# Second mixture layer: three quarters of its tiles in pairs, two raw-weight buffers, one ring of five PSUM banks

## The chip, the cores and the metric

The kernel runs on one core of a Trainium2 chip. The metric is the device time of one execution in microseconds. Before the change three runs gave 902.35, 903.67 and 905.14 us, so the median is 903.67 us.

## The reference, cut to what matters

Three stages follow one another: a gated recurrent attention, a soft mixture of experts, and a second mixture. The change is in the second mixture and in the step that leads into it.

```python
def _moe2_ref(x, w_gate, w1, w2):        # x 3072x320, w1 8x320x1024, w2 8x1024x320
    logits = x @ w_gate
    P = np.exp(logits - logits.max())
    for _ in range(8):                   # Sinkhorn steps over rows and columns
        P /= P.sum(1, keepdims=True) + 1e-09
        P /= P.sum(0, keepdims=True) + 1e-09
        P *= N / E
    for e in range(E):                   # E = 8
        h = np.maximum(x @ w1[e], 0.0)
        out += P[:, e:e + 1] * (h @ w2[e])
```

## The kernel before, in words

x of the second mixture is itself a product of a 3072x32 matrix c with 32 slot rows, so x @ w1[e] is computed as c @ (slots @ w1[e]). The small product slots @ w1[e] is `s1_p` (its matmuls are in `col4`, L1016 and L1022, its PSUM tile is called pu). It is scaled by a power of two and split into float16 parts in the tile sst. The power of two comes from `pow2`, which needs the largest absolute value over all 128 partitions. For that one of two ways is used: an all-reduce on POOL (L1113), or two transfers on SP's queue, the column of 128 maxima to DRAM (col, L1108) and back as a row on all partitions (row, L1109), after which DVE reduces it (`pow2_b`, L1118 to L1126). `pow2_w` does it for the second weights w2, `pow2_s` for s1.

The 3072 rows of x are 24 tiles of 128 rows. For a tile, `z_` (L1508) computes a half of x @ w1[e] into a PSUM bank of the pool psz (3 banks). ACT takes relu of it into float16 (`hi_z`, L1514), DVE the float16 rest (`relu_with`, L1517). The product with w2[e] uses three float16 products: high by high, high by low, low by high.

There are three kinds of units, each a run of slots; a slot is a handful of matmuls of the unit (`consume`), and a `produce` step of a unit that comes later.

- `Old` (4 slots): the last four tiles of expert 0. Expert 0 itself runs in `g1`/`g2` before that, block by block, with the eight Sinkhorn steps beside it on DVE (`sinkhorn`, L1383 to L1398).
- `One` (4 slots): one tile, 24 matmuls of 320 columns (L1540), then one DVE addition into acc (L1560).
- `Two` (7 slots): two tiles i and j at once, by seven products of half size (12 matmuls of 160 columns each, 84 in all, L1635) instead of eight. It needs sums of blocks of h and of w2. Sums of h: ACT casts (`cast`, L1588), DVE sums (L1517 into tmr), one sum on POOL (L1594, from r21 and r22), and five low parts on POOL (`lo_s`, L1520). Sums of w2 per expert: four on POOL (`sum_w`, L1490), then `sum_h` on ACT and `sum_l` on POOL. The result is put together by `keep_m`, `drain_x`, `drain_z` and `drain_y` on DVE and a little ACT.

Per expert 1 to 7 the units are eight times `One, Two`, so 88 slots (PER). `LEAD` says how many slots ahead of its first slot a unit's z halves are produced, 14 for both kinds. In that time the h parts must be ready; opr (two buffers), tmr (one buffer of five parts) and chl (three buffers) hold them. PSUM: psz 3 banks, psy 3 banks (y of One, y of Two), psp 2 banks (x and z of Two, pu).

Beside the units, `plan(c, f)` puts the preparation of the next expert n at slots counted from the expert's first slot. load_w2 brings w2 to the one tile raw at slot 80 of the expert before; `amax` (DVE) at 5 to 9, `pow2_w` at 14 with `pow2_b` 16 slots later, `prep_a` (ACT, high part of w2, at 31 to 34), `prep_s` (ACT scales raw in place, L1712, and POOL takes the low part, L1713), sums of w2 at 54 to 77, s1 at 33 to 54, and `scale_p` (DVE, L1159, the 24 scaled gate weights of an expert) at 78. Expert 1 has no expert before it in this loop, so its preparation is given in `EXTRA`, beside expert 0's blocks, and its sums by `plan_sums(4, 1, ...)` beside the `Old` units. Expert 1's units also multiply acc by the gate weight of expert 0 (`first`, L1555, DVE).

PE, ACT, DVE and POOL run in the order of the program text; SP's queue is ordered by a planner. Each engine takes its instructions strictly in order and waits for data by semaphores.

Of the kernel before, what the change touches and what calls it, by code (L numbers as in the profile page):

```python
# [20 lines left out]
def mlstm_moe_kernel(  # L21
# [984 lines left out]
    psy = ctx.enter_context(tc.tile_pool(name="psy", bufs=3, space=PSUM, reuse_waits="tile"))  # L1006
    psp = ctx.enter_context(tc.tile_pool(name="psp", bufs=2, space=PSUM, reuse_waits="tile"))
# [86 lines left out]

    def pow2(e, a, mx, later=None):
# [4 lines left out]
        iv, sc = (wp.tile([P, 1], F32, tag=f"{n_}{a}", name=f"{n_}{a}", bufs=2) for n_ in ("iv", "sc"))  # L1100
# [13 lines left out]
        pow2_b(e, a, mr, iv, sc)  # L1114
# [99 lines left out]
    def s1_p(e):  # L1214
        tmp["s1"] = psp.tile([P, TB], F32, tag="p", name="pu2")[:, 0:FQ]
# [229 lines left out]
    EXTRA = {2: [(amax, 0)], 3: [(amax, 1)], 4: [(amax, 2)], 5: [(amax, 3)], 7: [(prep_1, 0)], 9: [(prep_1, 1)],  # L1445
             10: [(s1_c, 0), (s1_c, 1)], 12: [(s1_c, 2), (s1_c, 3)], 14: [(prep_1, 2)], 16: [(prep_1, 3)]}
# [129 lines left out]
    class Two(One):  # L1576
        slots, banks = 7, 4
# [36 lines left out]
        def consume(self, k, at):  # L1614
# [18 lines left out]
            for kp in range(KH):  # L1633
                for a, b in ((0, bh), (0, bl), (1, bh)):
# [3 lines left out]
                    )  # L1638
            if k == 2:
# [21 lines left out]
        def drain_y(self):  # L1661
# [15 lines left out]

    units = [Old(tt) for tt in range(TPB)]
    ones_, twos = 0, 0
    for e in range(1, E):  # L1680
        for i in range(0, NT, 3):
            units += [One(e, i, None), Two(e, i + 1, i + 2, twos)]
            units[-2].buf = ones_
            ones_, twos = ones_ + 1, twos + 1
    LEAD = {One: 14, Two: 14}
# [11 lines left out]
    PER = sum(u.slots for u in units[TPB:]) // (E - 1)  # L1697
# [5 lines left out]
    for tt in range(TPB):  # L1703
        st = (NB - 2) * TPB + tt
        plan(4 * tt + 3, sinkhorn, st)
        for op, kk in EXTRA.get(st, ()):
            plan(4 * tt + 3, op, 1, kk)

    def prep_s(e, kk):
        ks = slice(2 * kk, 2 * kk + 2)  # L1710
        t = src2[e][:, ks, :]
        nc.scalar.activation(out=t, in_=t, func=AF.Copy, scale=scw[e][1])  # L1712
        nc.gpsimd.tensor_tensor(out=wl[e][:, ks, :], in0=t, in1=wh[e][:, ks, :], op=ALU.subtract)  # L1713
# [112 lines left out]
```

## Time and profile before

| | us |
|---|---|
| median of three runs | 903.67 |
| the profiled execution, its own time | 898.99 |
| its span | 897.3 |
| PE busy | 862.9 (96%) |
| DVE busy | 716.1 (80%) |
| POOL busy | 588.9 (66%) |
| ACT busy | 558.1 (62%) |

Busy time is a union: where instructions of an engine overlap, it counts once. "Releaser" is what ended an engine's idle time. Expert 0's blocks run from about 207 to 269.5 us, the four `Old` units from 269.5 to 286.9 us, experts 1 to 7 from 286.9 us to the end. The granted TensorE clock is 0.997 of full speed (2.4 GHz) over the span.

### The profile page before, as it was taken

How to read it: one execution, taken by the hardware profiler on the slowest of the kernel's cores; microseconds unless marked ns; L12 is line 12 of the kernel's file. 1: busy time of each engine (PE TensorE's matmuls, PEld its weight loads, DVE VectorE, ACT ScalarE, POOL GpSimd, SP SyncE). 2: the span in 40 equal slices, each digit the busy share in tenths (PEclk: the TensorE clock that was granted, in tenths of full speed). 3: DMA queues.
4: the chain of work that ended last, by engine and by line, in shares of the span. 5: the costliest groups of instructions: out<-in, count | busy, mean ns of one | idle time of the engine just before them, and what ended most of it. 6: DMA issues, size and time to landing. Idle time of an engine off the chain costs nothing.

```text
span 897.3 us, 26669 instructions
## 1 busy us (share of the span) xinstructions
PE 862.9 (96%) x10996; PEld 728.8 (81%) x10996; DVE 716.1 (80%) x1534; ACT 558.1 (62%) x1110; POOL 588.9 (66%) x596
## 2 busy tenths in 40 slices
PE   7999997899998989999999999999999999999997
PEld 5878884356676878888999899989889998988996
DVE  7777875455899989897788788878987897888774
ACT  7656653353245567668766776687577767767662
POOL 5766660000014679967996799689769977997663
PEclk9999999999999999999999999999999999999999
DMA  8999999960100121204110201051100110000111
GB/s 170 173 199 185 191 248 323 326 182 1 55 6 30 31 57 26 60 2 39 45 60 2 66 16 61 5 64 45 31 5 10 40 31 5 19 1 31 46 46 60
DMA packets 136402, 67.11 MB, mean 75 GB/s; under 512 B 105209, under 2 KB 130041, under 8 KB 136281
## 3 DMA queue, kind: packets, MB, share of 16 engines
q1 hardware_dynamic: 136009, 64.92, 30.1%
q8 instruction: 86, 1.41, 0.7%
q14 instruction: 35, 0.29, 0.2%
q10 hardware_dynamic: 224, 0.30, 0.1%
q0 software_dynamic: 48, 0.20, 0.1%
HBM read 60.17 MB, written 5.02 MB: 73 GB/s over the span
## 4 chain that ended last, share of the span: by engine, by line
PE 66%; DVE 10%; DMA 7%; POOL 7%; issue 5%; ACT 3%; SPq 1%; DVEq 0%; POOLq 0%; ACTq 0%
PE y L1540 15%; PE z L1508 6%; POOL op L1520 3%; DMA bigy<-in_moe_w_dram 3%; PE pss L432 2%; DVE tmr L1517 2%; PE ptk L383 2%; PE oa L477 2%; PE y L1312 2%; PE y L1313 2%; PE y L1314 2%; DMA wa<-in_moe_w_dram 1%; POOL raw L1490 1%; PE pe L402 1%; DVE acc L1560 1%
## 5 line engine op out<-in xcount | busy, mean ns | idle before, releaser
L1520 POOL TENSOR_TENSOR op<-tmr,op 128x512 f16<-128x512 f32 x280 | 319.1, 1168 | 22.1 <-ACT op L1588 19.0
L1635 PEld LDWEIGHTS <-op 128*128 128x128 f16 x4704 | 328.3, 98 | 0.6 <-issue 0.5
L1588 ACT CAST op<-tmr 128x512 f16<-128x512 f32 x280 | 170.0, 616 | 108.1 <-DVE tmr L1517 55.7
L1540 PE MATMUL y<-wx,ch 128*128 128x320 f16 x1344 | 219.0, 299 | 0.0
L1517 DVE SCALAR_TENSOR_TENSOR tmr<-z,tmr 128x512 f32<-128x512 f32 x168 | 114.7, 683 | 56.5 <-ACT op L1514 50.0
L1540 PEld LDWEIGHTS <-ch 128*128 128x128 f16 x1344 | 122.7, 98 | 35.0
L1508 PE MATMUL z<-cst,sst 96*128 96x128 f16 x1344 | 131.0, 219 | 11.7 <-DVE tmr L1517 4.9
L1594 POOL TENSOR_TENSOR tmr<-tmr 128x512 f32<-128x512 f32 x56 | 71.2, 1271 | 95.2 <-ACT tmr L1514 95.2
L1508 PEld LDWEIGHTS <-sst 96*128 96x128 f16 x1344 | 100.2, 98 | 33.6 <-issue 11.3
L1514 ACT ACTIVATE tmr<-z 128x512 f32<-128x512 f32 x112 | 64.8, 596 | 63.5 <-PE z L1508 51.7
L1517 DVE SCALAR_TENSOR_TENSOR ch<-z,ch 128x512 f16<-128x512 f32 x112 | 77.0, 688 | 18.1 <-ACT ch L1514 16.6
L1517 DVE SCALAR_TENSOR_TENSOR op<-z,op 128x512 f16<-128x512 f32 x112 | 76.2, 681 | 0.0
L1514 ACT ACTIVATE ch<-z 128x512 f16<-128x512 f32 x112 | 66.1, 591 | 2.8 <-PE my__8101 L1635 1.3
L1514 ACT ACTIVATE op<-z 128x512 f16<-128x512 f32 x112 | 66.6, 595 | 0.1
L1490 POOL TENSOR_TENSOR raw<-raw 128x640 f32<-128x640 f32 x28 | 43.8, 1565 | 8.3 <-DVE acc L1323 7.3
L1314 PE MATMUL y<-wh,hl 128*128 128x320 f16 x160 | 47.8, 299 | 0.3 <-DVE hl L1295 0.3
L1312 PE MATMUL y<-wh,hh 128*128 128x320 f16 x160 | 47.8, 299 | 0.0
L1313 PE MATMUL y<-wl,hh 128*128 128x320 f16 x160 | 47.8, 299 | 0.0
L411 ACT ACTIVATE dd<-pe 128x512 f32<-128x512 f32 x48 | 29.2, 609 | 29.4 <-PE pe L402 28.9
L1294 ACT ACTIVATE hh<-z 128x512 f16<-128x512 f32 x48 | 26.6, 595 | 33.1 <-PE z L1291 32.8
L1713 POOL TENSOR_TENSOR wx<-raw,wx 128x640 f16<-128x640 f32 x24 | 33.6, 1408 | 15.1 <-ACT raw L1712 15.1
L439 DVE TENSOR_TENSOR dd<-pss,dd 128x512 f32<-128x512 f32 x48 | 31.0, 685 | 14.7 <-PE pss L432 11.9
(1078 smaller groups left out, 1653.0 us busy)
## 6 DMA issues: line engine op xcount, KB each, us to landing
wa<-in_moe_w_dram SPq DMA_DIRECT2D x18, 512.0 KB
raw<-in_moe_w_dram SPq DMA_DIRECT2D x28, 320.0 KB
kq<-in_k_dram SPq DMA_DIRECT2D x24, 160.0 KB
kq<-in_q_dram SPq DMA_DIRECT2D x24, 160.0 KB
vz<-in_v_dram SPq DMA_DIRECT2D x24, 160.0 KB
xr<-in_o_gate_dram SPq DMA_DIRECT2D x24, 160.0 KB
wb<-in_moe_w_dram SPq DMA_DIRECT2D x6, 640.0 KB
out_dram<-acc SPq DMA_DIRECT2D x24, 160.0 KB
```

What stands on the lines that cost most here:

```text
L1312: nc.tensor.matmul(y, hh[:, kc, ts], wh[e][:, kc, :], start=(kc == 0), stop=False)
L1313: nc.tensor.matmul(y, hh[:, kc, ts], wl[e][:, kc, :], start=False, stop=False)
L1314: nc.tensor.matmul(y, hl[:, kc, ts], wh[e][:, kc, :], start=False, stop=(kc == KF - 1))
L1490: nc.gpsimd.tensor_tensor(out=quarter(*o), in0=quarter(*a), in1=quarter(*b), op=op)
L1508: nc.tensor.matmul(z[:, k, :], Sst[e][:, kc * P:(kc + 1) * P], cst[:, i * P:(i + 1) * P], start=True, stop=True,)
L1514: nc.scalar.activation(out=o, in_=z, func=AF.Relu)
L1517: nc.vector.scalar_tensor_tensor(out=o, in0=z, scalar=0.0, in1=x, op0=ALU.max, op1=op)
L1520: nc.gpsimd.tensor_tensor(out=o, in0=x, in1=h, op=ALU.subtract)
L1540: nc.tensor.matmul(self.y, self.at(a, kc), b[self.e][:, kc, :], start=(kc == a == 0 and b is wh), stop=(kc == KF - 1 and a == 1),)
L1588: cast = lambda m, x: nc.scalar.copy(out=hi(m), in_=x)
L1594: at(0, lambda: nc.gpsimd.tensor_tensor(out=s1_, in0=r21, in1=r22, op=ALU.add))
L1635: nc.tensor.matmul(t[:, c * DH:(c + 1) * DH], o[:, m, a, kp, :], b[kp], start=(kp == a == 0 and b is bh), stop=(kp == KH - 1 and a == 1),)
```

## The change

- Units: per expert `cPPcP` three times, where c is a One and P a Two, so 6 Ones and 9 Twos (87 slots); for the last expert `PPcPPPcPPPcPPc`, 4 Ones and 10 Twos. Before, every expert had 8 and 8. LEAD goes from 14 to 11.
- In every third Two the sum of r21 and r22 is made on DVE from z (L1517) and not on POOL. s4 takes the buffer of s1_, not that of r22.
- raw becomes two tiles, raws, taken in turn; m2w (first weights) gets a single tile. load_w2 is issued an expert earlier, `amax` and `pow2_w` of expert n + 1 run during the units of expert n - 1. Preparation slots are set anew.
- Expert 1's sums move into EXTRA beside expert 0's blocks and become like those of other experts (ACT and POOL, none on DVE); `prep_d` on DVE goes; maxima of expert 2 are taken there too.
- `scale_p` and `first` move from DVE to ACT.
- psy and psp are closed before the units and replaced by one pool of 5 banks in one ring.
- In `drain_y` the addition of y comes after the two `plus`.

```diff
     def load_w2(e):
-        src2[e] = raw
+        src2[e] = raws[e % 2]
...
         nc.gpsimd.partition_all_reduce(mr, mx, P, bass_isa.ReduceOp.max)
-        pow2_b(e, a, mr, iv, sc)
+        if (e, a) in SPLIT:                       # (1,0), (1,1), (2,1)
+            tmp["b", e, a] = lambda: pow2_b(e, a, mr, iv, sc)
+        else:
+            pow2_b(e, a, mr, iv, sc)
...
     def scale_p(e):
-        nc.vector.tensor_scalar(
-            out=Ps[:, :, e], in0=Pm[:, :, e], scalar1=sch[e][0], scalar2=scw[e][0], op0=ALU.mult, op1=ALU.mult,
-        )
+        for t, sc in ((Pm, sch[e][0]), (Ps, scw[e][0])):
+            nc.scalar.activation(out=Ps[:, :, e], in_=t[:, :, e], func=AF.Copy, scale=sc)
...
+    wa_ = ring_a.tile([P, WSL], F32, tag="w", name="wa")
+    raws = [ring_a.tile([P, WSL], F32, tag="w", name="raw2").rearrange("p (k d) -> p k d", d=DM), raw]
     load_m2w(1)
     load_w2(1)
+    load_w2(2)
...
-    EXTRA = {2: [(amax, 0)], 3: [(amax, 1)], 4: [(amax, 2)], 5: [(amax, 3)], 7: [(prep_1, 0)], 9: [(prep_1, 1)],
-             10: [(s1_c, 0), (s1_c, 1)], 12: [(s1_c, 2), (s1_c, 3)], 14: [(prep_1, 2)], 16: [(prep_1, 3)]}
+    EXTRA = {2: [(amax, 0), (amax, 1)], 3: [(amax, 2)], 4: [(amax, 3), (pow2_w,)], 5: [(amax_2, 0)],
+             6: [(b_, 1, 1), (b_, 1, 0), (amax_2, 1), (amax_2, 2)], 7: [(amax_2, 3), (pow2_2,)],
+             8: [(prep_a, 0), (prep_s, 0)], 9: [(prep_a, 1), (prep_s, 1), (s1_c, 0)],
+             10: [(prep_a, 2), (prep_s, 2), (s1_c, 1), (b_, 2, 1)], 11: [(prep_a, 3), (prep_s, 3), (s1_c, 2)],
+             12: [(sum_w, 0), (sum_w, 1), (s1_c, 3)], 13: [(sum_w, 2), (sum_w, 3)],
+             14: [(sum_h, 0), (sum_h, 1)], 15: [(sum_h, 2), (sum_h, 3), (sum_l, 0), (sum_l, 1)],
+             16: [(sum_l, 2), (sum_l, 3)]}
...
-            if n == 3 and tt == 0:
+            if n == 2 and tt == 1:
                 s1_p(1)
...
         def first(self, i):
-            if self.e == 1:
-                nc.vector.tensor_scalar_mul(acc[:, i, :], acc[:, i, :], Ps[:, i, 0:1])
+            a = acc[:, i, :]
+            nc.scalar.activation(out=a, in_=a, func=AF.Copy, scale=Ps[:, i, 0:1])
...
-            s4 = r22
+            s4 = s1_
...
-                at(0, lambda: nc.gpsimd.tensor_tensor(out=s1_, in0=r21, in1=r22, op=ALU.add))
+                if self.buf % 3 == 1:
+                    at(0, lambda: relu_with(s1_, z, r22, ALU.add))
+                else:
+                    at(0, lambda: nc.gpsimd.tensor_tensor(out=s1_, in0=r21, in1=r22, op=ALU.add))
...
+    LAST = "PPcPPPcPPPcPPc"
+        for c in "cPPcP" * 3 if e < E - 1 else LAST:
...
-    LEAD = {One: 14, Two: 14}
+    LEAD = {One: 11, Two: 11}
...
-            plan(c + 80, load_w2, n + 1)
+            plan(c + 2, load_w2, n + 1)
             plan(c + 36, load_m2w, n + 1)
+            plan(c + 35, pow2_w, n + 1, lambda *f, c=c: steps(c + 35, f))
         for kk in range(4):
-            plan(c + ((5, 6, 8, 9) if e > 1 else (10, 11, 12, 13))[kk], amax, n, kk)
-            plan(c + 31 + kk, prep_a, n, kk)
-            plan(c + (32, 33, 43, 44)[kk], prep_s, n, kk)
-        plan(c + 14, pow2_w, n, lambda *f, c=c: steps(c + 14, f))
-        plan_sums(c, n, (54, 55, 56, 65), (58, 59, 60, 69), (66, 67, 76, 77))
+            if n + 1 < E:
+                plan(c + (19, 20, 30, 31)[kk], amax, n + 1, kk)
+            plan(c + (5, 6, 16, 17)[kk], prep_a, n, kk)
+            plan(c + (7, 8, 18, 19)[kk], prep_x, n, kk)
+            plan(c + (9, 10, 20, 21)[kk], prep_y, n, kk)
+        plan_sums(c, n, (38, 39, 49, 50), (41, 42, 52, 53), (67, 68, 78, 79))
         plan(c + 33, s1_p, n)
-        plan(c + 34, s1_v)
-        plan(c + 35, pow2_s, n, lambda *f, c=c: steps(c + 35, f))
+        plan(c + 33, s1_v)
+        plan(c + 37, pow2_s, n, lambda *f, c=c: steps(c + 37, f))
         for k in range(3):
-            plan(c + 52 + k, s1_w, n, k)
-        plan(c + 78, scale_p, n)
+            plan(c + 54 + k, s1_w, n, k)
+        plan(c + 74, scale_p, n)
...
+    pctx.close()
+    psy = psp = Ring()
+    Ring.pool = ctx.enter_context(tc.tile_pool(name="psu", bufs=5, space=PSUM, reuse_waits="tile"))
```

Here `prep_x` is the scaling of `prep_s` on ACT, `prep_y` its subtraction on POOL, and `b_` runs a `pow2_b` that SPLIT had put off.

## Rows read from the trace of the kernel before

**Rows 1.** Windows of four stretches: us; busy us (instructions) of PE, PEld, DVE, ACT, POOL; clock; DMA.

```profile
200.00:269.50 69.50, 69.22 (x509) 47.93 (x507) 54.18 (x128) 27.38 (x54) 4.15 (x5) 1.00 0.06 20
269.50:287.00 17.50, 15.26 (x134) 11.36 (x133) 16.09 (x29) 9.46 (x16) 7.54 (x6) 1.00 0.00 1
287.00:397.00 110.00, 101.77 (x1258) 89.65 (x1257) 101.33 (x195) 71.58 (x140) 85.74 (x71) 1.00 0.16 42
414.30:499.40 85.10, 85.10 (x1085) 76.77 (x1088) 69.70 (x146) 61.12 (x120) 72.13 (x61) 1.00 0.21 38
```

**Rows 2.** What PE waited for, 269.5 us to the end: us, times, longest.

```profile
PE z L1508 <- DVE tmr L1517: 4.9, 4, 2.2
PE z L1508 <- DVE ch L1517: 4.3, 6, 1.3
PE z L1508 <- ACT tmr L1514: 2.0, 1, 2.0
```

**Rows 3.** PE's timeline, a One and a Two: start, us, line, tile, count.

```profile
425.36 0.98 PE L1540 MATMUL y<-wx,ch 128*128 128x320 f16 x6
426.17 0.39 PE L1508 MATMUL z<-cst,sst 96*128 96x128 f16 x4
...
429.53 0.99 PE L1635 MATMUL mx__6686<-wx,op 128*128 128x160 f16 x12
430.36 1.82 PE L1635 MATMUL mx__6686<-wt,op 128*128 128x160 f16 x24
...
435.80 0.98 PE L1540 MATMUL y<-wx,ch 128*128 128x320 f16 x6
```

**Rows 4.** Groups by line, one expert: count | busy us, mean ns | idle before.

```profile
L1520 POOL TENSOR_TENSOR op<-tmr,op 128x512 f16<-128x512 f32 x40 | 45.1, 1161 | 1.1 <-ACT op L1588 1.0
...
L1588 ACT CAST op<-tmr 128x512 f16<-128x512 f32 x40 | 24.2, 615 | 12.0 <-POOL tmr L1594 7.3 <-DVE tmr L1517 4.5
...
L1517 DVE SCALAR_TENSOR_TENSOR tmr<-z,tmr 128x512 f32<-128x512 f32 x24 | 16.4, 684 | 10.3 <-ACT op L1514 9.4 <-POOL tmr L1594 0.8
...
L1594 POOL TENSOR_TENSOR tmr<-tmr 128x512 f32<-128x512 f32 x8 | 10.2, 1271 | 9.5 <-ACT tmr L1514 9.5
...
L1713 POOL TENSOR_TENSOR wx<-raw,wx 128x640 f16<-128x640 f32 x5 | 7.0, 1407 | 3.6 <-ACT raw L1712 3.6
...
L1490 POOL TENSOR_TENSOR raw<-raw 128x640 f32<-128x640 f32 x4 | 6.3, 1588 | 0.2
...
L1712 ACT ACTIVATE raw<-raw,sc 128x640 f32<-128x640 f32 x5 | 4.0, 823 | 0.0
```

**Rows 5.** Timelines of DVE and PE around 635 us.

```profile
630.44 4.74 DVE L1159 TENSOR_SCALAR Ps<-Pm,iv,iv 128x24 f32<-128x24 f32 x1
...
637.02 0.40 PE L1508 MATMUL z<-cst,sst 96*128 96x128 f16 x4 [0.95 <-DVE tmr L1517]
```

**Rows 6.** Single lines over the whole run: duration ns min/median/max, first and last start.

```profile
L1159 DVE TENSOR_SCALAR Ps<-Pm,iv,iv x8: 991/1278/4739, 278.5 to 801.7; 128x24 f32<-128x24 f32 x8
...
L1555 DVE TENSOR_SCALAR acc<-acc,Ps x24: 374/668/1339, 294.5 to 383.9; 128x320 f32<-128x320 f32 x24
...
L1398 DVE TENSOR_TENSOR Pm<-Pm,ca x8: 357/358/786, 224.5 to 277.7; 128x192 f32<-128x192 f32 x8
...
L1320 ACT COPY acc<-y x4: 426/426/431, 202.3 to 207.0; 128x320 f32<-128x320 f32 x4
```

**Rows 7.** Timeline of all engines at the end.

```profile
891.00 0.99 PE L1635 MATMUL my__14830<-wx,op 128*128 128x160 f16 x12
...
892.10 0.33 DVE L1663 TENSOR_TENSOR mz__14812<-my__14830,q 128x160 f32<-128x160 f32 x1 [2.05 <-PE my__14830 L1635]
...
893.86 0.81 SPq L1670 DMA_DIRECT2D out_dram<-acc  x2
```

**Rows 8.** SyncE's timeline in one expert: the two small transfers of a maximum.

```profile
418.17 0.32 SPq L1108 DMA_DIRECT2D col<-mxs  x1
...
426.15 0.32 SPq L1109 DMA_DIRECT2D row<-col  x1
```

More of the change, by code (lines that the diff above doesn't have):

```diff
@@ L1099, in pow2 @@
         mr = wp.tile([P, n], F32, tag=f"mr{a}", name=f"mr{a}", bufs=2)
[L1100 removed]
+        iv, sc = (wp.tile([P, 1], F32, tag=f"{n_}{a}", name=f"{n_}{a}", bufs=3) for n_ in ("iv", "sc"))
         if later:
@@ new lines, in prep_y, with prep_s, quarter @@
+    def prep_y(e, kk):
+        ks = slice(2 * kk, 2 * kk + 2)
+        nc.gpsimd.tensor_tensor(
+            out=wl[e][:, ks, :], in0=src2[e][:, ks, :], in1=wh[e][:, ks, :], op=ALU.subtract,
+        )
+    def prep_s(e, kk):
+        prep_x(e, kk)
+        prep_y(e, kk)
+    SK = [1, 3, 5, 7, 9, 11, 13, 15, 17]
+    DH = DM // 2
+    KH = KF // 2
+    wth, wtl = (xacc.tile([P, 2, 4, KH, DH], F16, tag=f"by{j}", name=f"wt{j}") for j in (2, 3))
+    def quarter(e, a, b):
+        return src2[e][:, a * KH:(a + 1) * KH, b * DH:(b + 1) * DH]
@@ new lines, in mlstm_moe_kernel, with sum_w, sum_h, sum_l @@
+    SUMS = [((0, 0), (0, 1), (0, 0), ALU.subtract), ((0, 1), (1, 1), (0, 1), ALU.subtract),
+            ((1, 1), (0, 0), (1, 1), ALU.subtract), ((1, 0), (1, 0), (1, 1), ALU.add)]
+    def sum_w(e, j):
+        o, a, b, op = SUMS[j]
+        nc.gpsimd.tensor_tensor(out=quarter(e, *o), in0=quarter(e, *a), in1=quarter(e, *b), op=op)
+    def sum_h(e, j):
+        nc.scalar.copy(out=wth[:, e % 2, j], in_=quarter(e, *SUMS[j][0]))
+    def sum_l(e, j):
+        nc.gpsimd.tensor_tensor(
+            out=wtl[:, e % 2, j], in0=quarter(e, *SUMS[j][0]), in1=wth[:, e % 2, j], op=ALU.subtract,
+        )
@@ L1448, in sinkhorn, with extra @@
+    def extra(st):
+        for op, *kk in EXTRA.get(st, ()):
+            op(1, *kk)
     def sinkhorn(st):
@@ L1522, in mlstm_moe_kernel @@
     class One:
-        slots, banks = 4, 2
+        slots, banks, tiles = 4, 2, 1
         def __init__(self, e, i, buf):
-            self.e, self.i, self.h = e, i, chl[buf % 3] if buf is not None else None
+            self.e, self.i, self.buf = e, i, buf
         def produce(self, k, at):
@@ L1536, in consume @@
                 self.y = psy.tile([P, TB], F32, tag="y", name="y")[:, 0:DM]
+                if self.e == 1:
+                    at(0, lambda: self.first(self.i))
             w = KF // self.slots
@@ L1576, in mlstm_moe_kernel @@
     class Two(One):
-        slots, banks = 7, 4
+        slots, banks, tiles = 7, 4, 2
         def __init__(self, e, i, j, buf):
@@ L1638, in consume @@
                     )
+            if e == 1 and k in (0, 3):
+                at(0, lambda: self.first(self.i if k else self.j))
             if k == 2:
@@ L1680, in mlstm_moe_kernel @@
     for e in range(1, E):
[L1681 to L1684, printed above, removed]
-    LEAD = {One: 14, Two: 14}
+        i = 0
+        for c in "cPPcP" * 3 if e < E - 1 else LAST:
+            if c == "c":
+                units.append(One(e, i, ones_))
+                ones_ += 1
+            else:
+                units.append(Two(e, i, i + 1, twos))
+                twos += 1
+            i += units[-1].tiles
+    PER = sum(u.slots for u in units if u.e == 1)
+    LEAD = {One: 11, Two: 11}
     starts, c = [], 0
@@ L1695, in mlstm_moe_kernel @@
     when = {}
-    PER = sum(u.slots for u in units[TPB:]) // (E - 1)
     base = TPB * Old.slots
@@ L1705, in mlstm_moe_kernel @@
         plan(4 * tt + 3, sinkhorn, st)
[L1706 to L1713, printed above, removed]
+        plan(4 * tt + 3, extra, st)
     def plan_sums(c, e, sums, his, los):
         for j in range(4):
-            plan(c + sums[j], sum_w, j)
+            plan(c + sums[j], sum_w, e, j)
             plan(c + his[j], sum_h, e, j)
             plan(c + los[j], sum_l, e, j)
-    plan_sums(4, 1, (0, 3, 6, 9), (2, 5, 8, 11), (3, 6, 9, 12))
     def s1_v():
```

60 lines of the change are left out of this document (24 added, 36 removed).

## The prediction

> **What bounds the kernel now.** I read the busy time by windows first, to see which engine fills which stage. Over one expert's length in the second layer PE is busy 85.10 of 85.10 us, POOL 72.13, DVE 69.70, ACT 61.12 [rows 1]. So the steady part is bound by TensorE. The start is not: in the four Old units PE is idle 17.5 - 15.26 = 2.2 us, and in the 110 us behind them, which are expert 1 and a little of expert 2, 110 - 101.77 = 8.2 us, with DVE busy 101.33 of 110 [rows 1]. Then the list of what PE waited for: nearly all of it is z, a PSUM bank that DVE or ACT had not emptied, 4.9 + 4.3 + 2.0 us [rows 2]. Of the 4.9 us two waits lie late: at 637.02 PE waits 0.95 us behind DVE, whose small scaling of 24 gate weights took 4.74 us at 630.44 [rows 5], and once more of that size after the last such scaling at 801.7 [rows 6]. Last the timeline, for the price of a unit on PE, and the end.
>
> **Columns on PE.** Six matmuls of a One take 426.17 - 425.36 = 0.81 us, so a One's 24 take 3.26 us; twelve of a Two take 430.36 - 429.53 = 0.83 us, so its 84 take 5.82 us [rows 3]. A One, a Two and their six z halves take 435.80 - 425.36 = 10.44 us, which leaves 0.23 us for a z half [rows 3]. The pairs go from 56 to 6 x 9 + 10 = 64, the Ones from 56 to 6 x 6 + 4 = 40; the z halves stay. That removes 16 x 3.26 = 52.2 us and adds 8 x 5.82 = 46.6 us: **-5.6 us**. A pair is 0.70 us cheaper than two Ones. An expert then takes PE 6 x 3.26 + 9 x 5.82 + 48 x 0.23 = 83.0, with the s1 product (85.10 - 8 x 10.44 = 1.6) 84.6 us.
>
> The row gives 69 ns for a matmul of 160 columns and 136 ns for one of 320 [rows 3]. The Trainium skill speaks against more pairs (TensorE: Matmul & The Clock Gate, "Back-to-back issue gap"): in a stream of weight loads and matmuls it puts the pace at about 81 ns for 128 columns and 131 ns for 512. Between these, as an estimate, 160 columns would cost 85 ns and 320 columns 106 ns, a pair 7.1 us against 5.1 us for two Ones, and eight more pairs +16 us. This trace does not agree, and its rows are the case's own matmuls, so I go by them.
>
> **The stalls at the start of the units.** Three loads leave DVE there. Expert 0's weight on acc (24 times 0.67 us in the median, up to 1.34 [rows 6]) goes to ACT, the low parts of expert 1's sums go to POOL and are made earlier, beside expert 0, and the low parts of its w2 go too. DVE's 101.33 us lose about 16 us by the first alone [rows 6], and it is left at the share it has in the steady part. The idle time that can go is 2.2 + 8.2 = 10.4 us. I leave 4.4 us of it or of new waits, **-6.0 us**, for three reasons:
> - ACT takes the 24 scalings. The trace has none of 128x320 from SBUF; the copy of 128x320 took 0.43 us and the scaling of 128x640 0.82 us [rows 6, 4], so 24 x 0.43 to 0.82 = 10 to 20 us; I take 0.50, nearer the copy with as many elements, 12 us. ACT's other change per expert is one Two (four relus at about the cast's 0.62, five casts of 0.615 [rows 4], two small copies) for two Ones (four relus), about +3.5 us. Expert 1 so has 61 + 3.5 + 12 = 77 of 84.6 us of ACT, more where the weights are prepared (slots 5 to 19). Queued behind a scaling are the relus that free z.
> - Expert 0's stage gets POOL work: 4 low parts of w2 at 1.41, 4 sums at 1.59 [rows 4] and 4 low parts like the first, 17.6 us between its steps 8 and 16, where POOL had 4.15 us in 69.5 [rows 1]. The Sinkhorn multiplication took 0.36 us beside an idle POOL and 0.79 beside a busy one [rows 6]. Twelve contended operations in four steps then cost DVE 0 to 12 x 0.43 = 5.2 us. DVE has 69.5 - 54.18 = 15.3 us free over this stage [rows 1], so the price on PE is 0, up to 5 if it falls in a full stretch. The four reductions for expert 2's maxima are paid by the four splits (`prep_d`) that leave; both are DVE operations on 128x640.
> - The new ring starts on banks that were just used. The first unit may wait for a copy to acc, about 0.5 us, once, as the ACT copy's 0.43 us is the nearest row [rows 6].
>
> The Trainium skill words the second point more strictly (SBUF — State Buffer, "Who interferes with whom"): DVE with two SBUF inputs or in its two-port mode and a GpSimd instruction lock each other out for a whole instruction. The 4.74 us of one 24-element scaling [rows 5] agrees; by this rule alone a Sinkhorn operation could lose a POOL instruction each time, the second rival below.
>
> **Scaling the gate weights on ACT** takes the 4.74 us instruction off DVE, and with it two waits of 0.95 us [rows 2, 5]: **-1.9 us**. On ACT two small instructions replace it; the nearest row above is 0.43 us each [rows 6], hidden in ACT's idle 20 us.
>
> **The end.** Now the last matmuls start at 891.00, DVE puts the pair together from 892.10, and the transfer out is issued at 893.86 [rows 7]. The two issues take 0.81 us, so the second is at 894.27, 2.17 us behind DVE's start. With a One last there is one addition of 320 columns, 0.33 us (the first of the pair's, on 160) to twice that, and one issue; the pair before it has 3.3 us of the One's matmuls for its own end. At 0.55 us that is **-1.6 us** (-1.5 to -1.8).
>
> **What the rest costs.** *POOL per expert*: 72.13 + 5 x 1.16 (one pair more) - 2 x 1.27 (six sums, not eight) [rows 4] = 75.4 of 84.6 us. In a stretch of two adjacent pairs (14 slots, 2 x 5.82 + 8 x 0.23 = 13.5 us) POOL has 10 x 1.16 + 1.27 = 12.9 us, and the w2 work lies in slots (9, 10, 20, 21 in each group of 29) where no pair's POOL work is due. *DVE*: a pair for two Ones and three sums more at 0.68 [rows 4], less the gate scaling, about +3 of 15 free us. s4 in the buffer of s1_ adds a wait: DVE's s4 now waits for POOL's low part of s1_, issued a slot earlier; behind it on DVE stand the next relus, for which PE's z waits. At 1.16 us on a POOL with no backlog, that is one slot. *LEAD 11*: opr's buffer is read to slot 7 of pair n, and pair n + 2 starts 18 slots behind it, 18 - 11 = 7: no wait. In the last expert (14 apart) each part is still read before it is rewritten. *The ring*: eleven tiles in 29 slots over five banks, each freed five or more slots before its turn. *Raw weights an expert ahead*: the preparation no longer stands behind its maximum. *SP's queue*: two maxima now go out two slots apart, with the first-weight loads between. A maximum took 426.15 - 418.17 = 8.0 us from col to row [rows 8] and has 16 slots, about 15 us. If they went strictly one behind the other the second would have its row at 16 us and DVE would stand for a few us; I take 0.
>
> **Sum.** -5.6 - 6.0 - 1.9 - 1.6 = -15.1 us. The profiled execution took 898.99, so 883.9. It was 4.7 us below the median of 903.67; applied to that, **888.6 us**. The likeliest case's own range is 881 to 894: all the idle time gone, -19.5, gives 884, and 3 us more come from gaps too small for the list; the two upper prices on ACT and in expert 0 give 894.
>
> **Rivals.**
> 1. *POOL sets the pace* (slower). POOL's waits in an expert are 9.5 us on the sum of r21 and r22 and 3.6 us on the scaled weights [rows 4]. They are waits for data just made, and might stay: 75.4 + 13.1 = 88.5 us per expert against 84.6 of PE. Six experts at 88.5, not 85.1, cost +20.4; with -1.6 at the end, -1.4 in the last expert and -6 at the start, 903.67 + 11.4 = 915. For it: adjacent pairs, s4 waiting on POOL, and LEAD shorter by three slots. Against: the sum that POOL waits for goes to DVE in the second of two pairs, and most of POOL's idle time now lies where it had nothing to do. It decides when POOL's idle time per expert must stay over 9.2 us. 13 in 100.
> 2. *Lock-out beside the Sinkhorn steps*. If each of 12 operations loses a POOL instruction, 12 x 1.41 = 17 us [rows 4], less the DVE time free in that half of expert 0's stage, about 8: +9 on PE: 898. For it: the 4.74 us [rows 5]. Against: POOL's work there is spread over nine steps of 3.7 us, and steps 10, 12 and 14 have no Sinkhorn operations. 12 in 100.
> 3. *The start stays as stalled as it was*, because ACT takes DVE's place: only -5.6 - 1.9 - 1.6 = -9.1 are left, 894.6. For it: 77 of 84.6 us of ACT, crowded into the slots of the preparation. Against: z comes in bursts of two to four halves with gaps of three slots or more, in which a backlog of 2 us is worked off. 15 in 100.
> 4. *No change*: 2 and 3 together, about 903. 6 in 100.
>
> The likeliest case has 54. The measurement cannot tell 0.3% (2.7 us) from no change. Faster by more than that: 54 + 15 + 12, less 2 for the upper edge of rival 2, is 79; within it: 6 + 2 = 8; slower: 13. The range from 880 to 903 leaves out rival 1 and the edges.
>
> **What would show it.** Right: PE busy over 99% from 290 us on, z waits of a few us in all, 64 pairs at 5.82 us, an expert period near 84.6 us, no DVE scaling of gate weights, the last transfer about 2 us behind the last matmul. Wrong: an expert period of 86 us or more with PE's z waiting on DVE's sums and those on POOL; L1386 or L1398 over 0.7 us beside POOL with PE idle before 270 us; DVE standing at `pow2_b` for a row.

## The result, and the profile after

The changed kernel takes 888.71 us (median of four runs, 887.14 to 891.81) against 904.23 us for the kernel before in the same comparison. The ratio is 0.9835 with a 95% interval of 0.9803 to 0.9868, so 15.5 us less. The forecast was 888.6 us. The time came out; several steps of the sum did not, and their errors cancelled, so the agreement to 0.1 us is luck. The profiled execution took 891.81 us (span 889.9), that of before 898.99.

The engines' totals of the kernel after, from the first part of its page:

```profile
PE 860.4 (97%) x11284; PEld 739.1 (83%) x11284; DVE 705.0 (79%) x1570; ACT 593.3 (67%) x1210; POOL 629.2 (71%) x632
```

PE's busy time fell by only 2.5 us, and ACT and POOL rose by 35 and 40 us. The totals don't tell where the time came from. The same four stretches as in [rows 1] do, in the kernel after (columns: stretch, its length, then busy us of PE, PEld, DVE, ACT, POOL with instruction counts, granted clock, DMA share, GB/s):

```profile
200.00:269.50 69.50, 67.12 (x479) 45.58 (x478) 57.06 (x130) 29.95 (x56) 13.20 (x12) 0.98 0.06 20
269.50:287.00 17.50, 17.48 (x144) 12.98 (x143) 11.88 (x26) 10.75 (x22) 8.86 (x7) 1.00 0.25 77
287.00:397.00 110.00, 105.63 (x1361) 96.16 (x1359) 86.03 (x182) 88.95 (x182) 92.77 (x79) 0.97 0.14 30
414.30:499.40 85.10, 84.93 (x1122) 77.99 (x1120) 72.58 (x154) 64.03 (x128) 75.70 (x63) 1.00 0.15 38
```

Row by row: beside expert 0 PE now idles 2.4 us, and the clock is under 1. In the Old units the idle 2.2 us are gone. In expert 1's stretch PE still idles 4.4 us, though DVE fell from 101.33 to 86.03 us, and the granted clock is 0.97. In the steady part PE is as full as before, and POOL has 75.70 us where the forecast said 75.4.

What PE waited for from 260 to 890 us in the kernel after (total us, times, longest), which answers to [rows 2]:

```profile
PE z L1540 <- DVE tmr L1549: 5.3, 4, 4.1
PE z L1300 <- DVE hl L1304: 2.3, 1, 2.3
PE z L1540 <- DVE ch L1549: 0.9, 1, 0.9
```

There are fewer waits than before, and two are new: one of 4.1 us in expert 1's units and one of 2.3 us in expert 0's blocks.

**The 4.1 us.** SP's queue in the kernel after (start, us, engine, line, instruction, count):

```profile
323.95 0.33 SPq L1111 DMA_DIRECT2D col<-iv  x1
331.97 0.33 SPq L1112 DMA_DIRECT2D row<-col  x1
332.40 2.29 SPq L1111 DMA_DIRECT2D col<-mxs  x1
342.21 0.32 SPq L1112 DMA_DIRECT2D row<-col  x1
```

The first column is the maximum of expert 3's w2, which nobody needs yet; the second (from mxs) is that of expert 2's s1. SP takes its instructions in order, so the second column, whose maximum DVE had ready at 326.45, stands behind the first row, which waits 8 us for the first column. Its own issue then lasts 2.29 us where the first column's took 0.33; what held it is not clear from the trace. The urgent row is issued at 342.21. DVE and PE in the same stretch (in brackets the idle time before, and what ended it):

```profile
347.12 0.28 DVE L1124 TENSOR_REDUCE iv<-row 128x1 f32<-128x128 f32 x1 [6.81 <-DMA row<-col]
347.90 0.69 DVE L1549 SCALAR_TENSOR_TENSOR tmr<-z,tmr 128x512 f32<-128x512 f32 x1
```

```profile
344.80 0.98 PE L1574 MATMUL y<-wx,ch 128*128 128x320 f16 x6
349.84 0.61 PE L1540 MATMUL z<-cst,sst 96*128 96x128 f16 x4 [4.06 <-DVE tmr L1549]
350.24 1.81 PE L1574 MATMUL y<-wx,ch 128*128 128x320 f16 x6
```

DVE stands 6.81 us for the row with the rest of its work queued behind, and PE, which needs DVE to empty a z bank, stands 4.06 us. Then the same six matmuls take 1.81 us where they took 0.98. The windows around them name it: the granted clock is 1.00 ahead of the wait and 0.50 behind it, the lower of the two levels (1.2 GHz). By these rows 5.8 us at half pace cost another 2.9 us, as an estimate.

```profile
338.00:345.70 7.70, 7.70 (x111) 7.28 (x108) 2.21 (x7) 3.97 (x8) 5.09 (x4) 1.00 0.01 3
349.84:355.60 5.76, 5.46 (x28) 3.33 (x29) 5.37 (x13) 4.74 (x11) 4.65 (x5) 0.50 0.20 61
```

In later experts both columns go out ahead of both rows, and the wait is absent.

**The 2.3 us.** POOL beside expert 0's blocks in the kernel after:

```profile
245.17 0.38 POOL L1116 PARTITION_ALL_REDUCE mr<-mx  x1 [13.81 <-DVE mx L1091]
252.32 5.59 POOL L1454 TENSOR_TENSOR wx<-raw,wx 128x640 f16<-128x640 f32 x4 [6.77 <-ACT wx L1149]
257.87 6.51 POOL L1475 TENSOR_TENSOR raw<-raw 128x640 f32<-128x640 f32 x4
```

The fourth of the four low parts by itself, and the scaling on ACT that it reads:

```profile
256.51 1.40 POOL L1454 TENSOR_TENSOR wx<-raw,wx 128x640 f16<-128x640 f32 x1
255.61 0.83 ACT L1450 ACTIVATE raw<-raw,sc 128x640 f32<-128x640 f32 x1
```

DVE and PE in the same stretch, and the window behind PE's wait (columns as above):

```profile
256.56 1.56 DVE L1407 TENSOR_TENSOR Pm<-Pm,ca 128x192 f32<-128x192 f32 x1
258.55 1.01 DVE L1393 TENSOR_SCALAR rw<-rw 128x24 f32<-128x24 f32 x1
259.93 1.43 DVE L1395 TENSOR_TENSOR Pm<-Pm,rw 128x192 f32<-128x192 f32 x1
```

```profile
263.58 0.56 PE L1300 MATMUL z<-cst,sst 96*128 96x512 f16 x1 [2.31 <-DVE hl L1304]
263.58:267.00 3.42, 3.42 (x14) 2.17 (x14) 3.29 (x8) 0.98 (x2) 0.80 (x1) 0.51 0.00 0
```

Eight of the twelve operations that the forecast spread over nine steps ran back to back from 252.3 to 264.4 us. POOL had done nothing for 6.8 us behind its all-reduce, but that is not why: the scaling that the fourth low part needs ended at 256.44, POOL began that part at 256.51, so it had caught up, and it then ran the four sums, whose data were there, one behind the other. One Sinkhorn step of DVE fell on the fourth low part and the first sums: 1.56, 1.01 and 1.43 us where they take 0.36, 0.18 and 0.36 beside an idle POOL. That is 3.1 us more, PE waited 2.31, and again half the clock follows (0.51 over 3.4 us).

The end in the kernel after, which answers to [rows 7]:

```profile
885.18 0.81 SPq L1708 DMA_DIRECT2D out_dram<-acc  x2
886.60 0.55 DVE L1593 SCALAR_TENSOR_TENSOR acc<-y,Ps,acc 128x320 f32<-128x320 f32 x1 [0.99 <-PE y L1574]
887.18 0.33 SPq L1595 DMA_DIRECT2D out_dram<-acc  x1
```

From the last matmul to the end of the span it is 3.4 us, 5.3 before.

### The profile page after: what moved, and what is told of

The parts are those of the page before. It is cut to its first block, busy times and chain, and to the rows that moved or that the text cites. A ratio compares the mean times of both kernels' runs of the same rounds, so it can differ in the third digit from the quotient of the medians.

```text
span 889.9 us, 27440 instructions
## 1 busy us (share of the span) xinstructions
PE 860.4 (97%) x11284; PEld 739.1 (83%) x11284; DVE 705.0 (79%) x1570; ACT 593.3 (67%) x1210; POOL 629.2 (71%) x632
## 4 chain that ended last, share of the span: by engine, by line
PE 74%; DMA 11%; DVE 10%; ACT 3%; issue 2%; POOL 1%; SPq 0%; ACTq 0%; DVEq 0%
PE y L1574 14%; PE z L1540 7%; DMA bigy<-in_moe_w_dram 3%; PE pss L432 2%; DMA col<-mxs 2%; PE oa L477 2%; PE ptk L383 2%; DVE tmr L1549 2%; PE y L1321 2%; PE y L1322 2%; PE y L1323 2%; DMA wa<-in_moe_w_dram 1%; PE pe L402 1%; PE ob L488 1%; DVE op L1549 1%
## 5 line engine op out<-in xcount | busy, mean ns | idle before, releaser
L1552 POOL TENSOR_TENSOR op<-tmr,op 128x512 f16<-128x512 f32 x320 | 365.1, 1165 | 49.9 <-ACT op L1621 47.6
L1671 PEld LDWEIGHTS <-op 128*128 128x128 f16 x5376 | 376.6, 98 | 4.6 <-issue 2.9
L1621 ACT CAST op<-tmr 128x512 f16<-128x512 f32 x320 | 195.4, 617 | 43.3 <-DVE tmr L1549 37.0
L1549 DVE SCALAR_TENSOR_TENSOR tmr<-z,tmr 128x512 f32<-128x512 f32 x213 | 144.8, 682 | 52.5 <-ACT op L1546 39.4
L1574 PE MATMUL y<-wx,ch 128*128 128x320 f16 x960 | 152.9, 302 | 0.0
L1574 PEld LDWEIGHTS <-ch 128*128 128x128 f16 x960 | 89.4, 98 | 28.6
L1549 DVE SCALAR_TENSOR_TENSOR op<-z,op 128x512 f16<-128x512 f32 x128 | 86.9, 679 | 0.0
L1630 POOL TENSOR_TENSOR tmr<-tmr 128x512 f32<-128x512 f32 x43 | 54.7, 1272 | 28.8 <-ACT tmr L1546 24.1
L1549 DVE SCALAR_TENSOR_TENSOR ch<-z,ch 128x512 f16<-128x512 f32 x80 | 53.6, 683 | 6.7 <-ACT ch L1546 6.7
L1546 ACT ACTIVATE ch<-z 128x512 f16<-128x512 f32 x80 | 45.4, 592 | 4.2 <-PE z L1540 4.2
L1481 POOL TENSOR_TENSOR wt<-raw,wt 128x640 f16<-128x640 f32 x28 | 38.8, 1407 | 7.6 <-ACT wt L1478 7.6
```

What stands on the lines that cost most here:

```text
L1546: nc.scalar.activation(out=o, in_=z, func=AF.Relu)
L1549: nc.vector.scalar_tensor_tensor(out=o, in0=z, scalar=0.0, in1=x, op0=ALU.max, op1=op)
L1552: nc.gpsimd.tensor_tensor(out=o, in0=x, in1=h, op=ALU.subtract)
L1574: nc.tensor.matmul(self.y, self.at(a, kc), b[self.e][:, kc, :], start=(kc == a == 0 and b is wh), stop=(kc == KF - 1 and a == 1),)
L1621: cast = lambda m, x: nc.scalar.copy(out=hi(m), in_=x)
L1671: nc.tensor.matmul(t[:, c * DH:(c + 1) * DH], o[:, m, a, kp, :], b[kp], start=(kp == a == 0 and b is bh), stop=(kp == KH - 1 and a == 1),)
```

## The experiments

All are edits of the changed kernel unless said otherwise. To compare the profiles, each span is cut at three points: the first second-layer matmul of expert 0, the first of expert 1, and the end of the last matmul. "Stage 0" is the first stretch (expert 0 and the Old units), "units" the second (experts 1 to 7); times in us, worked out from the traces:

| kernel | median, ratio to before (95%) | span | stage 0 | units |
|---|---|---|---|---|
| before | 904.23 | 897.3 | 99.5 | 605.1 |
| b1_before | (one run: 904.47) | 902.7 | 99.5 | 609.0 |
| b2_before | (one run: 901.94) | 900.2 | 99.5 | 608.5 |
| after | 888.71, 0.9835 (0.9803 to 0.9868) | 889.9 | 101.1 | 598.5 |
| c0_after | 890.24, 0.9858 (0.9828 to 0.9888) | 888.5 | 98.1 | 597.6 |
| e1_row | 883.98, 0.9778 (0.9748 to 0.9807) | 883.8 | 98.4 | 591.6 |
| e2_psum | 887.43, 0.9820 (0.979 to 0.985) | 887.4 | 97.1 | 598.8 |
| e3_both | 882.02, 0.9769 (0.9741 to 0.9797) | 882.1 | 97.1 | 592.3 |
| c1_both | 882.43, 0.9765 (0.9738 to 0.9793) | 885.4 | 97.1 | 592.2 |
| e4_pairs | 883.68, 0.9775 (0.9748 to 0.9802) | 881.9 | 97.1 | 594.3 |
| e5_dve | 889.06, 0.9834 (0.9806 to 0.9861) | 890.2 | 97.1 | 599.9 |
| e6_s1pool | 883.70, 0.9777 (0.975 to 0.9804) | 882.0 | 97.1 | 592.8 |
| e7_rings | 884.67, 0.9787 (0.9733 to 0.9841) | 882.9 | 96.9 | 595.6 |
| e8_last | 882.36, 0.9764 (0.9718 to 0.981) | 880.5 | 97.1 | 592.0 |

c0 to e3 ran on one chip together, c1 to e6 on a second, e7 to b2 on the first again.

**c0_after**, the changed kernel once more, beside the next three.

> The changed kernel once more, as the yardstick for the runs beside it. If what cost it time in its first profile is in its program, PE again waits about 4 us for z behind DVE near 350 us (DVE stands over 5 us at the maximum's row) and about 2 us before 270 us, and the ratio to the kernel before is 0.98 to 0.987. If these two were chance, one or both are missing and the time is 4 to 7 us lower.

It took 890.24 us. The wait for the row is there again (PE 3.2 us, and half the clock behind it); expert 0's wait is only 0.9 us. There the same three operations of DVE took 0.42, 0.87 and 1.31 us. So the first wait comes back with the program, and the size of the second depends on how the two engines happen to fall together.

**e1_row** starts the maximum that is not urgent at slot 39, behind the urgent one, so that both columns go out ahead of both rows, and lets DVE reduce its row at slot 70 only. In the kernel after DVE reduced that row at 339.02 without a wait; the stand of 6.81 us was for the other.

```
-            plan(c + 35, pow2_w, n + 1, lambda *f, c=c: steps(c + 35, f))
+            plan(c + 39, pow2_w, n + 1, lambda f, g, c=c: (plan(c + 39, f), plan(c + 70, g)))
```

> The maximum of w2 starts its two transfers at slot 39, behind those of s1, and is used 31 slots later, so that nothing stands on the queue between the column and the row of s1's maximum. Theory (the row of s1's maximum was late because the queue waited for the column of w2's maximum first): DVE's stand of 6.8 us near 347 us goes, PE's 4.1 us wait and the half-clock stretch behind it (about 2.4 us) go, and the kernel takes 4 to 7 us less than the changed kernel beside it. Rival (the row was slow by chance, or the 8 us from column to row is what it takes whatever stands before it): DVE's wait stays in place or turns up elsewhere, within 1.5 us of the changed kernel.

883.98 us, 6.3 us less than c0_after. SP's queue in this kernel:

```profile
327.27 0.33 SPq L1111 DMA_DIRECT2D col<-mxs  x1
328.16 0.80 SPq L1111 DMA_DIRECT2D col<-iv  x1
335.05 1.26 SPq L1112 DMA_DIRECT2D row<-col  x2
```

```profile
340.46 0.29 DVE L1124 TENSOR_REDUCE iv<-row 128x1 f32<-128x128 f32 x1
```

The urgent row is issued 7.2 us earlier than in the kernel after, DVE has not to wait for it, and the units take 591.6 us, not 597.6 (c0_after). The queue's order is shown to be the cause.

**e2_psum** keeps the row and column factors of the Sinkhorn steps in PSUM, in the bank that holds the column sums, so that DVE's multiplications read one operand from SBUF and one from PSUM. POOL's work is as in the kernel after.

```
+        r = rw if pt is None else pt[:, 2 * E:2 * E + NT].unsqueeze(2)
...
+        ca = pt[:, E:2 * E]
```

> From the second Sinkhorn step on, the row and column factors are held in the PSUM bank of the step's matmul, so each of DVE's multiplications has one SBUF operand instead of two. Theory (DVE is locked out by POOL's twelve w2 operations because it reads two SBUF operands): the multiplications of 1.43 and 1.56 us beside POOL fall to about 0.4 us, the 1.01 us scaling to about 0.2, PE's 2.3 us wait before 270 us and the slow clock behind it (1.4 us) go: 2 to 4 us less than the changed kernel. Rival (DVE is late there because of the maxima of two experts and the split of s1): the multiplications' length stays or does not matter, and PE's wait stays within 1 us of what it was.

887.43 us, 2.8 less than c0_after, with intervals that overlap. The same three operations beside a busy POOL, on DVE in this kernel:

```profile
257.84 0.35 DVE L1409 TENSOR_TENSOR Pm<-Pm,psk 128x192 f32<-128x192 f32 x1
258.63 0.19 DVE L1394 TENSOR_SCALAR psk<-psk 128x24 f32<-128x24 f32 x1
259.20 0.35 DVE L1396 TENSOR_TENSOR Pm<-Pm,psk 128x192 f32<-128x192 f32 x1
```

They are back at 0.35, 0.19 and 0.35, no wait of PE is left ahead of 270 us, and stage 0 takes 96.9 to 97.1 us in this and every later kernel. That is 2.4 less than before, about the Old units' 2.2. Between the two profiled executions stage 0 falls by 1.0 us, against the kernel after by 4.0; the rest of the 2.8 is not found in a trace.

**e3_both** joins the two edits, **c1_both** is the same kernel beside the next three.

> Both edits together. If both theories hold the gains add, 6 to 11 us less than the changed kernel, and PE is idle under 3 us between 270 and 880 us. If the stalls only moved, the sum falls short of the two by more than 2 us.

> The kernel with both mends again (maximum of w2 later on the queue, Sinkhorn's factors in PSUM), as the yardstick for the three runs beside it: 880 to 884 us, ratio to the kernel before 0.974 to 0.980.

882.02 and 882.43 us. The first, timed beside c0_after, is 8.2 less, where the single edits gave 6.3 + 2.8 = 9.1. The two stalls are separate and, within the noise, add. This version beats both kernels.

**e4_pairs**: both mends, with the pattern of before (eight Ones and eight Twos per expert, 56 pairs in all).

```
-    LAST = "PPcPPPcPPPcPPc"
+    LAST = "cPcPcPcPcPcPcPPc"
-        for c in "cPPcP" * 3 if e < E - 1 else LAST:
+        for c in "cP" * 8 if e < E - 1 else LAST:
```

> Both mends, and the share of pairs as it was: 8 Ones and 8 Twos in every expert, one after the other, the last expert with a One at its end; 56 pairs, not 64. Theory (TensorE's columns bound the units): eight pairs at 5.82 us give way to sixteen Ones at 3.26, +5.6 us by the prediction's sum; by the expert periods of the two first traces (85.05 and 84.67 us) and 1.4 us in the last expert rather +3.7. Rival (two pairs side by side cost in waits what they save in columns): within 1 us of the yardstick or faster.

883.68 us, 1.3 over c1_both, with intervals that overlap; the units take 2.1 us more than in c1_both and 2.0 more than in e3_both. The theory (3.7 to 5.6 us) missed; the rival (within 1 us) is not excluded by the medians, and by the units it missed too. Taken from the median interval behind each kind of matmul (the s1 products as they took), the matmuls alone cost 589.8 us here and 584.0 with 64 pairs, so the columns are worth 5.8 us. What the units take beyond that (waits, and matmuls at the lower clock) is 4.5 us here and 8.4 in e3_both. PE's waits, e4_pairs and then e3_both:

```profile
PE z L1542 <- ACT tmr L1548: 0.8, 1, 0.8
```

```profile
PE z L1542 <- DVE ch L1551: 0.9, 1, 0.9
PE my__13079 L1673 <- issue: 0.8, 1, 0.8
PE my__5154 L1673 <- issue: 0.6, 1, 0.6
PE z L1542 <- DVE tmr L1551: 0.6, 1, 0.6
```

The new pattern gives back more than half of what its columns save, most of it around the seam to the last expert. Experts 2 to 5 take 84.67 us in e3_both and 85.22 to 85.29 here, so 0.6 us of the 0.70 arrives. Expert 6 takes 86.9 us in e3_both and 86.1 in c1_both, but 85.05 here, and the last expert is 0.6 us shorter than here where its columns are worth 1.4. Not all of this is the pairs': e3_both's waits without a releaser (my, `issue`, 1.4 us) lie partly elsewhere in c1_both, are absent from e6_s1pool, and stand in the kernel before too.

**e5_dve**: both mends, with `first` and `scale_p` on DVE again.

```
-            nc.scalar.activation(out=a, in_=a, func=AF.Copy, scale=Ps[:, i, 0:1])
+            nc.vector.tensor_scalar_mul(a, a, Ps[:, i, 0:1])
```

(and `scale_p` as one `nc.vector.tensor_scalar`, as before).

> Both mends, and the scalings of the gate weights and of acc back on DVE. Theory (they were the load that made DVE late at the start of the units, and POOL locks them out): +4 to +8 us, of it about 2 us by the scaling of the gate weights in later experts, the rest in expert 1, where PE waits for z behind DVE. Rival (the stalls at the start came from expert 1's sums of w2 on DVE and from late weights, which are mended anyway; DVE has room for the scalings): within 2 us of the yardstick.

889.06 us, 6.6 over c1_both. PE's waits, and the scalings on DVE from 287 to 375 us (busy us, mean ns):

```profile
PE z L1543 <- DVE ch L1552: 4.5, 6, 1.3
PE z L1543 <- DVE tmr L1552: 3.4, 3, 1.6
```

```profile
L1592 DVE TENSOR_SCALAR acc<-acc,Ps 128x320 f32<-128x320 f32 x23 | 17.7, 768 | 0.0
```

Expert 1 takes 92.0 us here and 85.3 in c1_both, experts 2 to 4 take 84.66 to 84.67 us in both. So the loss is `first`, and `scale_p` on DVE, for which 2 us had been expected, costs nothing at its new place: its longest takes 1.16 us, and PE does not wait behind it.

**e6_s1pool**: both mends, with the sum of r21 and r22 on POOL in every pair (`if self.buf % 3 == 1:` becomes `if False:`).

> Both mends, and the sum of two half tiles on POOL in every pair, as before the change. POOL gets three sums more per expert, 76.0 + 3 x 1.27 = 79.8 of 84.7 us. Theory (the units are bound by TensorE and POOL has room): 0 to +2 us. Rival (POOL's chain is what sets the pace as soon as pairs stand side by side): POOL's 79.8 us and 6 to 9 us of its waits pass 84.7 us, +1 to +4 us in each of six experts, +6 to +24 us in all.

883.70 us, 1.3 over c1_both with intervals that overlap; the units take 592.8 us, 0.6 more. POOL gets three more sums per expert and PE hardly notices: POOL does not set the pace.

**e7_rings**: both mends, with the two separate rings of before (psy 3 banks, psp 2) in place of the ring of five.

> Both mends, and the five PSUM banks again as two rings, three for y and two for the other products. Theory (every bank is free five slots before its turn in either way): the stretch from the first matmul of expert 1 to the last matmul stays within 0.5 us of 592.3 us. Rival (pairs side by side need the common ring): PE waits for the first product of a pair, +2 us or more.

884.67 us, 2.3 over e8_last, which ran beside it, with intervals that overlap; the units take 3.3 us more than in e3_both. That had been put at nothing. PE and DVE where it happens:

```profile
794.83 1.82 PE L1673 MATMUL mx__13842<-wt,op 128*128 128x160 f16 x24
799.00 1.00 PE L1673 MATMUL mz__13897<-wt,op 128*128 128x160 f16 x12 [2.12 <-DVE acc L1714]
800.22 1.81 PE L1673 MATMUL my__13923<-wx,op 128*128 128x160 f16 x12
```

```profile
794.21 1.29 DVE L1551 SCALAR_TENSOR_TENSOR tmr<-z,tmr 128x512 f32<-128x512 f32 x2 [0.76 <-POOL op L1554]
797.94 1.01 DVE L1714 SCALAR_TENSOR_TENSOR acc<-mz__13757,Ps,acc 128x320 f32<-128x320 f32 x2
```

Three pairs stand in a row at the seam to the last expert. With two banks a pair's third tile (mz) needs the bank of the mz of the pair before it, which DVE empties late, at 797.94, since it had waited for POOL. PE stands 2.12 us and loses more behind it at half the clock (1.81 for twelve matmuls that took 1.00). In e3_both, with five banks, DVE is as late (it waits the same 0.76 us and comes to that addition at 801.20), and PE has begun the third tile at 799.98 without a wait.

**e8_last**: both mends, and in the last expert nine pairs, never three in a row.

```
-    LAST = "PPcPPPcPPPcPPc"
+    LAST = "PPcPcPPcPcPPcPc"
```

> Both mends, and the last expert with at most two pairs side by side (PPcPcPPcPcPPcPc: 9 pairs and 6 Ones, not 10 and 4). Theory (three pairs in a row are more than DVE keeps up with: waits of 0.7, 0.3 and 1.0 us stand in the last 90 us): the waits go, a pair less costs 0.7 us of columns, the stretch from the first matmul of expert 1 to the last matmul shortens from 592.3 us by about 1 us; the timed difference is inside the noise, -3 to +1. Rival (the waits belong to the start of the last expert and not to the triples): +0.7 us in that stretch.

882.36 us and units of 592.0, against 882.0 to 882.4 and 592.3 with the old LAST: no difference that these runs can tell. The small waits at the start of the last expert stay (PE's z, 0.56, 0.11 and 0.87 us, from 792 to 804 us), so they don't come from the triples inside it. They lie at the seam, which this edit leaves as it was. The first goes back to POOL: DVE stood 2.53 us for a low part,

```profile
791.79 0.69 DVE L1551 SCALAR_TENSOR_TENSOR tmr<-z,tmr 128x512 f32<-128x512 f32 x1 [2.53 <-POOL op L1554]
```

and POOL was busy without a gap over 0.1 us from 782 to 796 us, with two low parts of w2's sums (L1484, 786.76 and 789.25, the steps of slots 78 and 79) among the pairs' own. No run moves these two, so this is read from the trace and not tested; the cause of the last wait is open.

**b1_before, b2_before**: the kernel before, two more profiles.

> The kernel before, for a second profile of it. The first profile took 899 us where its timed runs have 904. Theory (executions differ by some us in the stages that are limited by transfers, ahead of expert 1): expert 1 starts at 288 to 294 us, not 286.9, and the stretch behind it is again 605 us. Rival (the units themselves vary): that stretch is 607 us or longer, with more waits for z in expert 1.

> The same once more, as a third profile: the same two readings.

The forecast's profile was a low one. Units take 609.0 and 608.5 us here, 605.1 there. The difference has two parts. The first is gate weights on DVE. In b1_before, DVE and then PE:

```profile
548.67 4.72 DVE L1159 TENSOR_SCALAR Ps<-Pm,iv,iv 128x24 f32<-128x24 f32 x1
```

```profile
555.24 0.40 PE L1508 MATMUL z<-cst,sst 96*128 96x128 f16 x4 [1.80 <-DVE tmr L1517]
```

Such a wait follows the scaling in four experts of each of these two executions (0.9 to 1.9 us each, 4.6 and 4.8 us in all), and in two of the forecast's, 1.9 us in all [rows 5, 6]. The second is the clock. All three profiles of before have the same wait of 2.04 us for ACT in expert 1, near 330 us. It ends at 329.86 us in the forecast's profile and at 331.42 in b1_before. The stretch from 333 to 336 us in these two, in this order (columns as in the windows above):

```profile
333.00:336.00 3.00, 3.00 (x48) 3.00 (x46) 2.88 (x6) 1.14 (x3) 3.00 (x3) 1.00 0.39 38
```

```profile
333.00:336.00 3.00, 3.00 (x25) 3.00 (x24) 2.88 (x5) 2.50 (x5) 3.00 (x4) 0.50 0.03 6
```

Forty-eight matmuls in one, 25 in the other. The expectation that the variation lay ahead of expert 1 fell for the most part: expert 1 starts at 288.5 and 286.4 us, against 286.9, and the units vary by more.

## Why the forecast was right, and where it was not

**Columns, -5.6: right in the matmuls.** These alone go from 589.6 to 584.0 us, and a pair still takes seven times 0.83 us. An undisturbed expert goes from 85.05 to 84.67 us (forecast 84.6), so of the 0.70 us that the prices give, 0.38 arrive: two z halves that start 0.24 and 0.09 us late (599.5 and 600.8 us in e3_both) are the 0.3 us between.

**The end, -1.6: right**, 1.9.

**Stalls at the start, -6.0 with 4.4 left over: right on what goes, wrong on what comes.** The Old units' 2.2 us are gone, and with both mends expert 1 takes 84.7 to 85.5 us (e8_last, e7_rings) where it took 93.1, so the 4.4 us left over were too much. Taking `first` off DVE is worth some 6 us (e5_dve), and ACT carries it without a wait, at 0.558 us each where 0.50 was taken. What came in its place is the next two points.

**SP's queue, "I take 0": the step that failed.** The sentence in the forecast names the mechanism, two maxima strictly one behind the other, and DVE standing for a few us, and then prices it at nothing because the row has 16 slots. Sixteen slots are 15 us; the row was reduced 23 us behind the first column's issue, and DVE, idle for 6.8 us, put PE to a stand of 4 us and into the lower clock. e1_row measures the price, 6.3 us. The trace had the number that was needed: 8.0 us for one maximum [rows 8], twice that for two in line, and no slack for loads between them.

**Expert 0's POOL work, 0 of 0 to 5: too small.** It costs 1.0 to 4.0 us on PE (stage 0 of 98.1 to 101.1 against 97.1), 2.8 in the medians, within their noise (e2_psum). "DVE has 15.3 us free over this stage" was an average; the free time was not where POOL's operations ran. Rival 2 had the mechanism and over-priced it: not all twelve operations, but one step's, lost a POOL instruction each.

**Gate weights on ACT, -1.9: too small for a usual execution.** The two waits of the forecast's profile were four in each of the next two, 4.6 and 4.8 us. And the gain is not ACT's alone: in the changed kernel, with its new slot, the same instruction on DVE costs nothing (e5_dve). The forecast asked only where it ran, and not what it met on POOL; that this decides is argued, as no run moved the slot by itself.

**The new ring, 0.5 for its first wait: not found.** There is no such wait. In its place the ring gives 2 to 3 us that the forecast left out, by covering a late DVE (e7_rings; the waits are in the trace, the medians' intervals overlap).

**Rival 1, POOL sets the pace: fell.** POOL's busy time is as worked out and still leaves 9.4 us of idle time per expert, of which 8.6 are waits for ACT:

```profile
POOL op L1552 <- ACT op L1621: 6.1, 9, 1.8
POOL tmr L1630 <- ACT tmr L1546: 2.5, 3, 1.3
```

The rival let such waits put 88.5 us on an expert. They stayed, and the expert took 84.67: what POOL waits for is early enough for PE, but at the seam to the last expert (e8_last). Rival 3 was right that the start stays stalled, but not by ACT.

**The range.** Its upper end, 894, lies 5.4 us above the forecast, which is expert 0's upper price of 5.2 alone; the price on ACT that is named beside it is not in it.

**Why the sum still came out.** Without the two new stalls, what the units take beyond their matmuls falls from 15.4, 19.4 and 18.9 us (the three profiles of before) to 8.4 (e3_both). With the Old stall that is about 12 us, where the forecast had 6.0 + 1.9 = 7.9. The two new stalls give 8.2 of it back (e3_both against c0_after), where it had 0.5 inside the 4.4. In the spans, a mean of 900.1 falls to 889.2, by 10.9; the timed medians fall by 13.7 and 15.5. Some 3 to 5 us of these lie in executions that were not profiled, and nothing here tells where. So the time was hit because stalls that went were priced too low and stalls that came at nothing. The profile told the two apart where the time could not: two of the forecast's own signs of being wrong came true, DVE standing at `pow2_b` for a row (6.81 us) and Sinkhorn multiplications over 0.7 us beside POOL with PE idle ahead of 270 us (1.43 and 1.56 us, 2.31 us of PE).

## What to carry to other kernels

On a queue that runs in order, count two dependent transfers as two round trips: put what starts both ahead of what waits for either, and let the one that nobody needs yet go last. A free share over a whole stage says nothing about an operation that meets another engine's block of work; read the few microseconds in which they meet. A stall of 2 to 4 us on PE cost half as much again and more in clock in most of the traces here. Profile the kernel before more than once before a term is read from its waits: here one of three profiles had half of those behind the gate weights.

## What was not expected of the hardware

- **POOL behind an all-reduce.** Between `PARTITION_ALL_REDUCE` (ended at 245.55) and POOL's next operation lie 6.8 us in the kernel after, and 6.8 to 7.6 us in the eleven profiles of it and its edits, though ACT had made the inputs 0.6 us before the all-reduce ended (at 245.0 in the kernel after). The gap of 7.3 us at this place in the kernel before is not the same: there POOL waited for DVE's L1147, which ended at 252.08. In the kernel after, PE lost nothing by it: POOL had caught up at its fourth operation, which began 0.07 us behind its input. In the others it began 0.1 to 0.8 us behind.
- **A PSUM operand ends the lock-out.** With the factors in PSUM the same DVE operations on 128x192 take 0.35 us beside a busy POOL, and 1.43 to 1.56 with both operands in SBUF. The 128x24 addition in place goes from 1.01 to 0.19. The Trainium skill (SBUF — State Buffer, "Who interferes with whom") says that a DVE instruction with at most one SBUF input, outside its two-port modes, does not contend with GpSimd; these numbers agree.
- **The clock behind a stall.** In the kernel after, waits of 4.06 and 2.31 us are followed by stretches at a granted clock of 0.50 and 0.51 (5.8 and 3.4 us long). The wait of 1.80 us in b1_before is not: the twelve matmuls behind it, at 555.47, take 1.00 us. And the same wait of 2.04 us in the kernel before was followed by the full clock in one execution and by the lower in two. So what a stall costs differs from one execution to the next.
